# A spatial bias folded into the matmul sum, gating read from PSUM on VectorE, and two buffers moved

## The chip, the cores and the metric

The kernel runs on one core of a Trainium2 chip. The metric is the device time of one execution in microseconds (us); lower is better. The engines are TensorE (PE in the rows, its weight loads PEld), VectorE (DVE), ScalarE (ACT), GpSimd (POOL) and SyncE (SP), which issues nearly all DMAs. Each engine works through its own instructions in the order in which the program gives them.

## The reference, cut to what matters

An mLSTM attention over 2 batches of 768 tokens feeds a gated layer, and that a channel mix. The change is in the gated layer (bias and gating) and at the start of the channel mix:

```
h = np.maximum(x @ w_in, 0.0)
u, v = h[..., :512], h[..., 512:]
v_n = (v - mean) / np.sqrt(var + 1e-06)
v_s = np.einsum('ts,bsd->btd', w_spatial, v_n) + b_spatial[None, :, None]
x = (u * v_s) @ w_out                       # the gated layer's output
xk = mu_k * x + (1.0 - mu_k) * x_prev       # x_prev: x one token earlier
xr = mu_r * x + (1.0 - mu_r) * x_prev
k = np.maximum(xk @ w_k, 0.0)
out = sigmoid(xr @ w_r) * ((k * k) @ w_v)
```

## The kernel before

All products are made of rounded 32-bit pairs: a value is split into a high part and the rest (the low part), and a product is the sum of high by high, high by low and low by high. So each tensor on its way to TensorE needs a cast (ScalarE) and a subtraction of the cast (VectorE or GpSimd).

**Stages.** Until about 134 us attention, w_in products (`vp`, `up`) and normalising (`vn`) are interleaved. Then comes the stage of the change. The tokens are worked on in four groups g = 0 to 3 (batch b = g // 2, half hf = g % 2, 384 tokens each):

- `spatial(g, d)`, four times per group (d = 0 to 3): 18 products `spp` of 128x384 into one PSUM bank. They read `vn` of the batch and `wsp` of the half. Then VectorE adds the bias (L999) and so empties the bank, GpSimd multiplies by `u` (L1000), ScalarE casts (L1001) and VectorE subtracts; the results are the two halves of a `gt` tile.
- `wout(g)`: 32 products `wop`, three result banks, which are copied into `x2_g` (L1017 to L1020). The result for f = 2 comes first, and its copy is L1018.
- `mixed(g, w, ...)`: the token mix of `x2_g` into a buffer `tm`, and its split into `xk` (w = 0) or `xr` (w = 1).
- `kpart(g, f, xk)`: 8 products `kp`, with a chain of ScalarE (relu), GpSimd (square), ScalarE (cast), VectorE (rest); then 24 products `rp` (sigmoid), then 72 products `vv`, and the output.

**Order on TensorE.** Line 1084 sets it: group 0's `spp`, group 1's, `wop` of 0, `spp` of 2, `wop` of 1, `spp` of 3, `wop` of 2, then 32 `kp` of group 0, `wop` of 3, 32 more `kp`, `rp`, `vv`, and then groups 1 to 3 of the channel mix.

**Order on the other engines.** A planner (`Chain`, `advance`, `issue`) issues the steps of each chain when its own clock says that they can start; the second entry of a step is its assumed length in us. Those numbers set only the order. The weights w_k, w_r, w_v and the second half of w_spatial come by DMA into a few raw slots, and are split there (`widen`: three VectorE steps, two of ScalarE, one of GpSimd per piece; a piece of w_spatial needs only a cast and a subtraction). The raw slots are two of tag `wraw`, and after attention one of the three `xt` slots.

**Buffers.** Twelve pages of tag `pg` hold in turn `vn`, `wk`, `x2_g` and `tm`: which page a new tile takes follows from the order in which the program asks for pages and gives them up, and its first writer waits until the last reader of the old tile is through. `gk` slots (11) hold `gt` and later `k2`. A `vn` of a batch is two pairs of pages: chunks 0 to 2, which the first nine of each 18 products read, and chunks 3 to 5.

Of the kernel before, what the change touches and what calls it, by code (L numbers as in the profile page):

```python
# [7 lines left out]
F32 = mybir.dt.float32  # L8
# [9 lines left out]
def tile_mlstm_gmlp_channelmix(  # L18
# [56 lines left out]
    done = {}  # L75
    back = []
    split = []
    raws = dict(wraw=0, xt=0)
    rawcap = dict(wraw=2, xt=0)
    owners = {}  # L80

    class Chain:
# [87 lines left out]
    def chain(key, *steps, ready=None):  # L170
        running.append(Chain(key, steps, clock[0] + 0.2 if ready is None else ready, 0.0))
# [59 lines left out]
    def sub(eng, out, a, b):  # L231
        eng.tensor_tensor(out=out, in0=a, in1=b.bitcast(F32), op=ALU.subtract)  # L232
# [9 lines left out]
    def raw_slot(n):  # L242
        tag = [t for t in raws if raws[t] < rawcap[t]][0]
        raws[tag] += 1
        return base.tile([P, 5 * 128 if tag == "xt" else 512], I64, tag=tag, name="wraw",
                         bufs=3 if tag == "xt" else 2)[:, :n], tag

    def widen(key, hi, lo, src=None, raw=None, ready=0.0):
        n = (raw if src is None else src).shape[-1]
        u = n / 512.0  # L250
        t = {}
        me = (key, next(ids))

        def fetch():
            t["raw"], t["tag"] = raw_slot(n)
            load_end[0] = load(t["raw"], src, n)

        def low():
            for o, sl in lo if isinstance(lo, tuple) else ((lo, slice(0, n)),):
                sub(pool, o, t["sq"][:, sl], hi[:, sl])  # L260
            split.remove(me)

        def s1():
            split.append(me)
            pair = (t["raw"] if raw is None else raw).bitcast(I32).rearrange("p (n two) -> p n two", two=2)
# [25 lines left out]
    def rows3(t, w):  # L291
        return t[:, :3 * w].rearrange("p (a b) -> p a b", a=3)
# [682 lines left out]
    sync.dma_start(out=b_sb, in_=b_sp)  # L975
    x2 = {}
    gts = {}

    def run(prs, out, after, first=(), cost=0.16):
        for t in mm3([out], prs, after, first, cost):  # L980
            t[0]()

    def spatial(g, d):
        b, hf = divmod(g, 2)
        prs = []
        for s in range(NCH):
# [17 lines left out]
        run(prs, mm_bank(f"spp{g}_{d}", ("sp", g, d))[:, :HF], after, [f"w_sp{hf}"] + [("vn", NCH * b + s) for s in range(NCH)])  # L1004
# [88 lines left out]
    def kpart(g, f, xk):  # L1093
        sl = slice((f % 4) * P, (f % 4 + 1) * P)

        def after(ps):
            own("sq", 3, ("k2", g, f))
            sq = rk.tile([P, HF], F32, tag="sq", name=f"sq{g}_{f}", bufs=3)
            t = gated(f"k2_{g}_{f}")
            chain(("k2", g, f), ("A", 0.37, lambda: act.activation(out=sq, in_=ps, func=AF.Relu), ("kp", g, f)),  # L1100
                  ("P", 0.96, lambda: pool.tensor_tensor(out=sq, in0=sq, in1=sq, op=ALU.mult)),  # L1101
                  ("A", 0.41, lambda: act.copy(t[:, 0], sq)), ("V", 0.47, lambda: sub(vec, t[:, 1], sq, t[:, 0])))  # L1102
            k2t[g, f] = t

        run(pairs320(xparts(xk, slice(0, HF)), wparts(wk[f // 4], sl), swap=True),
            mm_bank(f"kp{g}_{f}", ("kp", g, f))[:, :HF], after, [("mx", g, 0), f"w_k{f // 4}"])

    xk = xks[0]
    for g in range(2 * B):
# [8 lines left out]
        for j in range(3):  # L1118
            sl = slice(j * P, (j + 1) * P)
            own("rs", 3, ("ob", g, j))  # L1120
            rs = r2.tile([P, DM], F32, tag="rs", name=f"rs{g}_{j}", bufs=3)
            run(pairs320(xparts(xr, sl), wparts(wr, slice(0, DM))), mm_bank(f"rp{g}_{j}", ("rs", g, j))[:, :DM],
                lambda ps, rs=rs, j=j: chain(("rs", g, j), ("A", 0.35, lambda: act.activation(out=rs, in_=ps, func=AF.Sigmoid))),
                [("mx", g, 1), "wr"], 0.133)
            rss.append(rs)
        for j in range(3):
            sl = slice(j * P, (j + 1) * P)
# [6 lines left out]
            def after(ps):  # L1134
# [113 lines left out]
```

## Time and profile before

| | us |
|---|---|
| median of 3 runs | 331.29 (330.44 to 336.69) |
| profiled execution, own time | 327.45 |
| its span, first to last instruction | 325.7 |
| TensorE busy in the span | 302.4 |
| VectorE, ScalarE, GpSimd busy | 224.3, 163.2, 145.6 |

The profiled execution is one run of its own; it was 3.84 us under the median of the three timed runs. Busy time of TensorE counts the overlap of its pipelined products, so a stretch in which it is always busy can still be slow where the granted clock is low.

### The profile page before, as it was taken

What the parts mean: (1) busy time and instruction counts of PE and PEld (TensorE: products, weight loads), DVE (VectorE), ACT (ScalarE), POOL (GpSimd) and SP (SyncE); (2) the same over time, 40 slices, a digit from 0 to 9 for tenths busy, and PEclk for the clock granted to TensorE, in tenths of its full rate; (3) what the DMA queues carried; (4) which work ended last, traced back from release to release, by engine and by line L of the source; (5) the groups of instructions that cost most, each with busy time, mean ns of one, the idle gap of its engine ahead of it and who ended that gap; (6) DMA issues with size and microseconds to landing.
All of it is one profiled execution on the core that took longest, in us unless ns stands there. A gap on an engine that the chain in (4) does not pass through costs nothing.

```text
span 325.7 us, 5486 instructions
## 1 busy us (share of the span) xinstructions
PE 302.4 (93%) x1982; PEld 281.5 (86%) x1982; DVE 224.3 (69%) x430; ACT 163.2 (50%) x336; POOL 145.6 (45%) x185
## 2 busy tenths in 40 slices
PE   5979988999999999899999999449999999999995
PEld 3676866989989989799999999339999999999995
DVE  6679698958689656654997929996565745645611
ACT  4542644685466342742455316458874844753620
POOL 4133457935758644853464631655502502501500
PEclk9969997999999999999999999987999999999999
DMA  5763942353443213244115211410001001001001
GB/s 181 248 174 124 344 135 85 109 169 105 163 132 112 84 49 104 89 155 139 42 40 193 83 40 40 122 42 2 0 22 41 2 20 40 2 20 42 0 20 42
DMA packets 12854, 28.97 MB, mean 89 GB/s; under 512 B 2099, under 2 KB 6187, under 8 KB 12827
## 3 DMA queue, kind: packets, MB, share of 16 engines
q1 hardware_dynamic: 12795, 28.56, 27.5%
q8 instruction: 16, 0.26, 0.3%
q14 instruction: 11, 0.09, 0.1%
q0 software_dynamic: 32, 0.07, 0.1%
HBM read 26.35 MB, written 1.97 MB: 87 GB/s over the span
## 4 chain that ended last, share of the span: by engine, by line
PE 74%; DVE 10%; ACT 5%; POOL 4%; DMA 3%; issue 2%; SPq 1%; DVEq 0%; ACTq 0%; POOLq 0%
PE spp L612 14%; PE vv L612 13%; PE kp L612 12%; PE vp L612 6%; PE wop L612 5%; PE up L612 5%; PE av L541 5%; PE rp L612 4%; PE sc L444 3%; DMA w_inv<-in_w_in_dram 2%; PE ld L453 2%; DVE wbits L274 2%; PE wp L348 2%; PE ip L525 2%; PE sp L491 1%
## 5 line engine op out<-in xcount | busy, mean ns | idle before, releaser
L1101 POOL TENSOR_TENSOR sq<-sq 128x384 f32<-128x384 f32 x32 | 27.2, 852 | 60.3 <-ACT sq L1100 60.3
L612 PE MATMUL spp<-wsp,vn 128*128 128x384 f32 x288 | 51.0, 335 | 1.5 <-POOL vn L232 0.9
L612 PEld LDWEIGHTS spp<-wsp,vn 128*128 128x128 f32 x288 | 49.8, 188 | 2.2 <-POOL vn L232 1.2
L612 PE MATMUL kp<-xk,wk 128*128 128x384 f32 x256 | 45.9, 336 | 4.6 <-DVE vs L999 4.6
L612 PEld LDWEIGHTS kp<-xk,wk 128*128 128x128 f32 x256 | 44.4, 188 | 5.2 <-DVE vs L999 5.2
L612 PE MATMUL vv<-wv,k 128*128 128x320 f32 x288 | 43.4, 310 | 0.1
L612 PEld LDWEIGHTS vv<-wv,k 128*128 128x128 f32 x288 | 42.4, 188 | 0.6 <-DVE k L232 0.3
L232 DVE TENSOR_TENSOR k<-sq,k 128x384 fp32r<-128x384 f32 x32 | 25.7, 802 | 21.7 <-ACT k L1102 21.7
L612 PE MATMUL vp<-w_v,xg 128*128 128x512 f32 x96 | 29.3, 422 | 2.3 <-ACT xg L603 1.4
L612 PE MATMUL up<-xg,w_u 128*128 128x256 f32 x192 | 31.2, 293 | 0.0
L612 PE MATMUL wop<-gt,wo 128*128 128x384 f32 x128 | 25.7, 358 | 4.5 <-DVE vs L999 2.9
L612 PEld LDWEIGHTS wop<-gt,wo 128*128 128x128 f32 x128 | 24.1, 203 | 5.7 <-ACT wv L285 3.2
L1000 POOL TENSOR_TENSOR vs<-vs,u 128x384 f32<-128x384 f32 x16 | 20.5, 1281 | 14.2 <-DVE vs L999 14.2
L612 PEld LDWEIGHTS up<-xg,w_u 128*128 128x128 f32 x192 | 26.2, 190 | 0.5
L541 PEld LDWEIGHTS av<-kvq,dt 128*128 128x128 f32 x192 | 25.7, 203 | 0.7
L541 PE MATMUL av<-kvq,dt 128*128 128x41 f32 x192 | 25.3, 284 | 0.0
L1100 ACT ACTIVATE sq<-kp 128x384 f32<-128x384 f32 x32 | 15.4, 491 | 15.4 <-PE kp L612 15.4
L274 DVE SCALAR_TENSOR_TENSOR wbits<-wsq,wbits 128x320 int32<-128x320 int32 (+1 forms) x27 | 21.3, 793 | 2.5 <-ACT wsq L269 2.1
L612 PEld LDWEIGHTS vp<-w_v,xg 128*128 128x128 f32 x96 | 17.5, 194 | 5.8 <-DVE xg L232 1.5
L466 DVE TENSOR_TENSOR dt<-dt,sc 128x512 f32<-128x512 f32 x24 | 16.2, 682 | 7.7 <-ACT dt L463 4.5
L1140 DVE TENSOR_TENSOR ob<-rs,vv 128x320 f32<-128x320 f32 x12 | 5.8, 487 | 20.7 <-PE vv L612 20.7
L463 ACT ACTIVATE dt<-ld 128x512 f32<-128x512 f32 x24 | 14.1, 597 | 9.2 <-PE ld L455 6.1
(160 smaller groups left out, 560.3 us busy)
## 6 DMA issues: line engine op xcount, KB each, us to landing
kvq<-in_kvq_dram SPq DMA_DIRECT2D x10, 516.0 KB
qk<-in_qk_dram SPq DMA_DIRECT2D x24, 160.0 KB
wraw<-in_w_k_dram SPq DMA_DIRECT2D x6, 512.0 KB
wraw<-in_w_v_dram SPq DMA_DIRECT2D x8, 320.0 KB
wraw<-in_w_sp_dram SPq DMA_DIRECT2D x12, 192.0 KB
og<-in_o_tok_dram SPq DMA_DIRECT2D x4, 480.0 KB
out_dram<-ob SPq DMA_DIRECT2D x12, 160.0 KB
w_inv<-in_w_in_dram SPq DMA_DIRECT2D x3, 512.0 KB
```

The source lines that it names most:

```text
L232: eng.tensor_tensor(out=out, in0=a, in1=b.bitcast(F32), op=ALU.subtract)
L274: vec.scalar_tensor_tensor(out=t["bits"], in0=t["sq"].bitcast(I32), scalar=3, in1=t["bits"], op0=ALU.logical_shift_left, op1=ALU.bitwise_or)
L348: pe.matmul(wp[:, :256], junk[:, :P], junk, start=True, stop=True)
L444: pe.matmul(st["sc", i, x][:, h * P:(h + 1) * P], k_[64 * x:64 * x + D, h, :], q_[64 * x:64 * x + D, h, :], start=True, stop=True)
L453: pe.matmul(ld, lts[c % 2][:, b], rl[:, hh * 512:(hh + 1) * 512], start=True, stop=not early)
L463: ("A", 0.48, lambda: act.activation(out=d2, in_=ld, func=AF.Exp), ("e", i, hh)),
L466: ("V", 0.6, lambda: vec.tensor_tensor(out=d2, in0=d2, in1=sc, op=ALU.mult)))
L541: pe.matmul(av[:, 4 * hh + h, :], A[:, h, :], vt[:, 4 * hh + h, :], start=True, stop=True)
L612: pe.matmul(out[0], l, x, start=j == 0, stop=j == len(prs) - 1)
L1000: ("P", 0.96, lambda: pool.tensor_tensor(out=vs, in0=vs, in1=ut[b][:, d, sl], op=ALU.mult)),
L1100: chain(("k2", g, f), ("A", 0.37, lambda: act.activation(out=sq, in_=ps, func=AF.Relu), ("kp", g, f)), ("P", 0.96, lambda: pool.tensor_ten ...
L1101: ("P", 0.96, lambda: pool.tensor_tensor(out=sq, in0=sq, in1=sq, op=ALU.mult)),
```

## The change

1. **Bias as a product.** `bm` (128 x 768) is a copy of the broadcast bias rounded by ScalarE; in its lower 64 partitions VectorE puts the rest (bias minus rounded bias). `sel` is a 128x128 tile of 1/64. One more product, `sel` by `bm`, ends the sum of each `spatial(g, d)`: 64 times 1/64 of the rounded bias plus 64 times 1/64 of the rest. There are 16 such products, 19 in each sum instead of 18.
2. **Gating on VectorE.** The bias addition (L999) and the multiplication on GpSimd (L1000) go; VectorE multiplies the PSUM bank by `u` instead.
3. **The mixing buffer.** `tm` of group 0, w = 0 takes the third `xt` slot instead of a page. Each page after it shifts by one: before, `x2_1` took the first page of batch 1's `vn`; now it takes a page of batch 0's `vn`, and `x2_2` the first page of batch 1's.
4. **The raw slot.** The third raw slot moves from tag `xt` to a slot of its own (`rraw`) in the pool `rk`, and takes the space of one `gk` slot (10 instead of 11). The bias arrives in a `gk` slot.
5. **Estimates.** The planner's assumed lengths are set to other numbers, and so the order on VectorE, ScalarE, GpSimd and SyncE shifts.

```
-    rawcap = dict(wraw=2, xt=0)
+    rawcap = dict(wraw=2, xt=0, rraw=0)
...
+        if tag == "rraw":
+            return late_pool[0].tile([P, 512], I64, tag=tag, name="wraw", bufs=1)[:, :n], tag
...
-        v = 0.06 + 0.54 * u
+        v = 0.06 + (1.06 if closing else 0.54) * u
...
-    rawcap["xt"] = 1
+    rawcap["xt"] = 0
...
+    rawcap["rraw"] = 1
...
-        return rk.tile([P, 2, HF], F32R, tag="gk", name=name, bufs=11)
+        return rk.tile([P, 2, HF], F32R, tag="gk", name=name, bufs=10)
...
-    b_sb = r1.tile([P, S], F32, name="b_sb")
+    b_sb = gated("b_sb").rearrange("p w t -> p (w t)").bitcast(F32)
+    bm = r1.tile([P, S], F32R, name="bm")
+    sel = r1.tile([P, P], F32R, name="sel")
     sync.dma_start(out=b_sb, in_=b_sp)
+    pool.memset(sel.bitcast(F32), 1.0 / 64)
+    act.copy(bm, b_sb)
+    sub(vec, bm[64:], b_sb[64:], bm[64:])
...
             prs += [(v0, w0), (v0, w1), (v1, w0)]
+        prs.append((sel, bm[:, hf * HF:(hf + 1) * HF]))
...
-                  ("V", 0.47, lambda: vec.tensor_tensor(out=vs, in0=ps, in1=b_sb[:, sl], op=ALU.add), ("sp", g, d)),
-                  ("P", 0.96, lambda: pool.tensor_tensor(out=vs, in0=vs, in1=ut[b][:, d, sl], op=ALU.mult)),
-                  ("A", 0.41, lambda: act.copy(gt[:, 0], vs)), ("V", 0.47, lambda: sub(vec, gt[:, 1], vs, gt[:, 0])))
+                  ("V", 0.55, lambda: vec.tensor_tensor(out=vs, in0=ps, in1=ut[b][:, d, sl], op=ALU.mult), ("sp", g, d)),
+                  ("A", 0.51, lambda: act.copy(gt[:, 0], vs)), ("V", 0.7, lambda: sub(vec, gt[:, 1], vs, gt[:, 0])))
...
-        t = rows3(page(f"tm{g}_{w}", F32, keys=[("mx", g, w)]), HF)
+        t = xslot(f"tm{g}_{w}", 3 * HF).bitcast(F32) if (g, w) == (0, 0) else page(f"tm{g}_{w}", F32, keys=[("mx", g, w)])
+        t = rows3(t, HF)
```

**Where the instructions stand.** The names in the rows are those of the program with buffer numbers behind; `spp_0` is the sum for d = 0, `x_1` is `x2_1`, `wop_2` the result for f = 2, `tm_0` the mixing buffer for w = 0. TensorE, end of the first sum of group 0 and start of the second, before:

```order
L612 MATMUL spp_0_1785<-wsp_1_1040,vn_0_1302 128x384 x2
L612 MATMUL spp_0_1785<-wsp_1_1040,vn_1_1303 128x384
L612 MATMUL spp_1_1821<-wsp_0_1039,vn_0_491 128x384 x2
L612 MATMUL spp_1_1821<-wsp_0_1039,vn_1_492 128x384
L612 MATMUL spp_1_1821<-wsp_0_1039,vn_0_491 128x384 x2
```

The same place on TensorE in the changed kernel:

```order
L616 MATMUL spp_0_1790<-wsp_1_1040,vn_0_1302 128x384 x2
L616 MATMUL spp_0_1790<-wsp_1_1040,vn_1_1303 128x384
L616 MATMUL spp_0_1790<-bm,sel 128x384
L616 MATMUL spp_1_1823<-wsp_0_1039,vn_0_491 128x384 x2
L616 MATMUL spp_1_1823<-wsp_0_1039,vn_1_492 128x384
```

The bias product stands between the first sum and the second. It waits for VectorE (`bm`) and for GpSimd (`sel`), and everything behind it on TensorE stands in its queue.

VectorE at the same time, before, from the last `vr` of the normalising to the first `gt`:

```order
L679 TENSOR_SCALAR vr_1708<-vr_1708,sb_1709 128x512
L232 TENSOR_TENSOR wsp_0_1783<-wraw,wsp_0_1783 128x384 x2
L999 TENSOR_TENSOR vs_0_1816<-spp_0_1785,b_sb 128x384
L232 TENSOR_TENSOR wsp_0_1783<-wraw,wsp_0_1783 128x384
L232 TENSOR_TENSOR wsp_1_1784<-wraw,wsp_1_1784 128x384 x2
L232 TENSOR_TENSOR gt_0_1817<-vs_0_1816,gt_0_1817 128x384
```

VectorE there in the changed kernel:

```order
L683 TENSOR_SCALAR vr_1708<-vr_1708,sb_1709 128x512
L233 TENSOR_TENSOR bm<-b_sb,bm 64x768
L233 TENSOR_TENSOR wsp_0_1788<-wraw,wsp_0_1788 128x384
L1016 TENSOR_TENSOR vs_0_1818<-spp_0_1790,u_841 128x384
L233 TENSOR_TENSOR wsp_0_1788<-wraw,wsp_0_1788 128x384 x2
L233 TENSOR_TENSOR gt_0_1819<-vs_0_1818,gt_0_1819 128x384
```

The rest of the bias is made right behind the last `vr`, ahead of all `wsp` pieces. On ScalarE the cast of `bm` stands likewise behind the last cast of `vn` and ahead of the `wsp` casts.

ScalarE around the copy of group 1's first `wop` result, before:

```order
L1001 CAST gt_2_2211<-vs_2_2210 128x384
L1037 ACTIVATE tm_0_2245<-x_0_2036,omu_sb 128x384 x2
L1018 COPY x_1_2246<-wop_2_2247 64x384
L1037 ACTIVATE tm_0_2245<-x_0_2036,omu_sb 128x384
L1001 CAST gt_3_2241<-vs_3_2240 128x384
L1020 COPY x_1_2246<-x_1_2246 64x384
L1017 COPY x_1_2246<-wop_0_2267 128x384
L269 ACTIVATE wsq<-wraw 128x320
L1044 CAST xk_2244<-tm_0_2245 128x1152
```

ScalarE there in the changed kernel:

```order
L1017 CAST gt_2_2204<-vs_2_2203 128x384
L272 ACTIVATE wsq<-wraw 128x512
L1055 ACTIVATE tm_0_2243<-x_0_2039,omu_sb 128x384 x2
L1034 COPY x_1_2244<-wop_2_2245 64x384
L1017 CAST gt_3_2239<-vs_3_2238 128x384
L1055 ACTIVATE tm_0_2243<-x_0_2039,omu_sb 128x384
L1033 COPY x_1_2244<-wop_0_2260 128x384
L1036 COPY x_1_2244<-x_1_2244 64x384
L1033 COPY x_1_2244<-wop_1_2279 128x384
L289 CAST wk_0_2100<-wsq 128x512
L1062 CAST xk_2242<-tm_0_2243 128x1152
```

The copy into `x_1` stands at nearly the same place in the queue; what has moved is its page, and with it the tile whose readers it waits for.

## Rows read from the trace of the kernel before

**Rows 1.** Busy time by stretch, all engines: PE, PEld, DVE, ACT, POOL, granted clock, DMA share.

```profile
185.00:196.00 11.00, 11.00 (x65) 11.00 (x64) 4.23 (x5) 2.73 (x6) 5.02 (x4) 1.00 0.17 54
196.00:212.00 16.00, 11.44 (x65) 10.80 (x64) 15.34 (x28) 8.85 (x18) 6.32 (x7) 1.00 0.28 82
```

**Rows 2.** Timeline of TensorE, 125 to 250: start, length, line, operation, count, [idle before, releaser].

```profile
138.75 22.30 PE L612 MATMUL spp<-wsp,vn 128*128 128x384 f32 x127 [0.87 <-POOL vn L232]
...
166.44 12.64 PE L612 MATMUL spp<-wsp,vn 128*128 128x384 f32 x72
178.92 5.71 PE L612 MATMUL wop<-gt,wo 128*128 128x384 f32 x32
184.46 12.64 PE L612 MATMUL spp<-wsp,vn 128*128 128x384 f32 x72
...
202.49 2.94 PE L612 MATMUL kp<-xk,wk 128*128 128x384 f32 x16
207.37 1.69 PE L612 MATMUL kp<-xk,wk 128*128 128x384 f32 x8 [1.95 <-DVE vs L999]
211.67 1.68 PE L612 MATMUL kp<-xk,wk 128*128 128x384 f32 x8 [2.61 <-DVE vs L999]
216.29 1.72 PE L612 MATMUL wop<-gt,wo 128*128 128x384 f32 x6 [2.94 <-DVE vs L999]
218.66 0.69 PE L612 MATMUL wop<-gt,wo 128*128 128x384 f32 x1 [0.64 <-ACT gt L1001]
220.27 6.19 PE L612 MATMUL wop<-gt,wo 128*128 128x384 f32 x25 [0.93 <-DVE gt L232]
...
231.84 3.67 PE L612 MATMUL rp<-wr,xr 128*128 128x320 f32 x24
```

**Rows 3.** Timeline of VectorE, 125 to 250.

```profile
195.92 0.55 DVE L1019 TENSOR_TENSOR x<-x,wop 64x384 f32<-64x384 f32 x1 [6.77 <-ACT x L1018]
...
202.65 0.56 DVE L999 TENSOR_TENSOR vs<-spp,b_sb 128x384 f32<-128x384 f32 x1
...
215.60 0.55 DVE L999 TENSOR_TENSOR vs<-spp,b_sb 128x384 f32<-128x384 f32 x1
```

**Rows 4.** Timeline of ScalarE, 125 to 250.

```profile
140.49 0.62 ACT L681 CAST vn<-vr 128x512 fp32r<-128x512 f32 x1 [1.88 <-DVE vr L679]
141.02 1.34 ACT L731 CAST wsp<-wraw 128x384 fp32r<-128x384 f32 x3
...
195.41 0.48 ACT L1018 COPY x<-wop 64x384 f32<-64x384 f32 x1 [6.69 <-PE spp L612]
```

**Rows 5.** Busy time by stretch around the bias load, columns as in Rows 1.

```profile
139.20:140.60 1.40, 1.40 (x10) 1.40 (x9) 0.95 (x1) 0.11 (x1) 1.40 (x3) 1.00 0.94 343
140.60:141.90 1.30, 1.30 (x9) 1.30 (x9) 0.34 (x1) 1.30 (x4) 0.75 (x2) 1.00 0.00 0
```

**Rows 6.** Timeline of SyncE's DMA issues, 134 to 143.

```profile
138.00 0.43 SPq L975 DMA_DIRECT2D b_sb<-in_b_sp_dram  x1
```

**Rows 7.** Timeline of GpSimd, 125 to 250.

```profile
141.19 1.31 POOL L232 TENSOR_TENSOR vn<-vr,vn 128x512 fp32r<-128x512 f32 x1 [0.55 <-ACT vn L681]
```

**Rows 8.** The tile wsp from 115 to 152: durations min/median/max in ns.

```profile
L232 DVE TENSOR_TENSOR wsp<-wraw,wsp x6: 546/554/1350, 141.6 to 147.8; 128x384 fp32r<-128x384 f32 x6
```

**Rows 9.** Groups of instructions, shapes kept apart: count, busy us, mean ns of one.

```profile
L1000 POOL TENSOR_TENSOR vs<-vs,u 128x384 f32<-128x384 f32 x16 | 20.5, 1281 | 14.2 <-DVE vs L999 14.2
...
L999 DVE TENSOR_TENSOR vs<-spp,b_sb 128x384 f32<-128x384 f32 x16 | 8.8, 548 | 0.1
L1001 ACT CAST gt<-vs 128x384 fp32r<-128x384 f32 x16 | 8.2, 511 | 12.0 <-POOL vs L1000 12.0
...
L1044 ACT CAST xk<-tm 128x1152 fp32r<-128x1152 f32 x4 | 4.6, 1157 | 2.3 <-DVE tm L1040 2.3
...
L232 DVE TENSOR_TENSOR xk<-tm,xk 128x768 fp32r<-128x768 f32 x4 | 3.8, 958 | 3.8 <-ACT xk L1044 3.7
```

**Rows 10.** Busy TensorE by stretch: length, PE busy, granted clock, DMA share.

```profile
53.10:56.50 3.40, 3.40 (x21) 0.50 0.01 3
...
216.90:220.30 3.40, 1.83 (x6) 0.50 0.02 7
220.30:223.70 3.40, 3.40 (x11) 0.50 0.00 0
```

More of the change, by code (lines that the diff above doesn't have):

```diff
@@ L77, in tile_mlstm_gmlp_channelmix @@
     split = []
-    raws = dict(wraw=0, xt=0)
-    rawcap = dict(wraw=2, xt=0)
+    raws = dict(wraw=0, xt=0, rraw=0)
+    rawcap = dict(wraw=2, xt=0, rraw=0)
+    late_pool = []
     owners = {}
@@ L281, in s3 @@
                 raws[t["tag"]] -= 1
-        v = 0.06 + 0.54 * u
-        steps = [("V", 0.12 + 0.54 * u, s1, None, lambda: len(split) < 2), ("V", v, s2), ("V", v, s3),
+        v = 0.06 + (1.06 if closing else 0.54) * u
+        steps = [("V", 0.12 + (0.84 if closing else 0.54) * u, s1, None, lambda: len(split) < 2), ("V", v, s2), ("V", v, s3),
                  ("A", 0.16 + 0.36 * u, lambda: act.copy(hi, t["sq"])), ("P", 0.1 + 1.13 * u, low)]
@@ L964, in tile_mlstm_gmlp_channelmix, with run @@
     at.release()
-    rawcap["xt"] = 1
+    rawcap["xt"] = 0
     rk = tc.alloc_tile_pool(name="rk", bufs=1, side="right", reuse_waits="tile")
+    late_pool.append(rk)
+    rawcap["rraw"] = 1
     def gated(name):
-        return rk.tile([P, 2, HF], F32R, tag="gk", name=name, bufs=11)
+        return rk.tile([P, 2, HF], F32R, tag="gk", name=name, bufs=10)
     r1 = tc.alloc_tile_pool(name="r1", bufs=1, side="right", reuse_waits="tile")
-    b_sb = r1.tile([P, S], F32, name="b_sb")
+    b_sb = gated("b_sb").rearrange("p w t -> p (w t)").bitcast(F32)
+    bm = r1.tile([P, S], F32R, name="bm")
+    sel = r1.tile([P, P], F32R, name="sel")
     sync.dma_start(out=b_sb, in_=b_sp)
+    pool.memset(sel.bitcast(F32), 1.0 / 64)
+    act.copy(bm, b_sb)
+    sub(vec, bm[64:], b_sb[64:], bm[64:])
+    use("A", 0.85)
+    use("V", 0.9)
     x2 = {}
     gts = {}
-    def run(prs, out, after, first=(), cost=0.16):
+    def run(prs, out, after, first=(), cost=0.173):
         for t in mm3([out], prs, after, first, cost):
@@ L1041, in blend @@
                                                     in1=t[:, c], op0=ALU.mult, op1=ALU.add)
-        chain(("mx", g, w), *[("A", 0.5, keep(c)) for c in range(3)], *[("V", 0.53, blend(c)) for c in range(3)],
-              ("A", 1.05, lambda: act.copy(xt[:, 0:3], t)),
-              ("V", 0.87, lambda: sub(vec, xt[:, 3:5], t[:, 0:2], xt[:, 0:2])),
+        chain(("mx", g, w), *[("A", 0.6, keep(c)) for c in range(3)], *[("V", 0.62, blend(c)) for c in range(3)],
+              ("A", 1.16, lambda: act.copy(xt[:, 0:3], t)),
+              ("V", 0.96, lambda: sub(vec, xt[:, 3:5], t[:, 0:2], xt[:, 0:2])),
               ("V", 0.47, lambda: sub(vec, xt[64:, 2], t[64:, 2], xt[64:, 2])),
@@ L1099, in after @@
             t = gated(f"k2_{g}_{f}")
-            chain(("k2", g, f), ("A", 0.37, lambda: act.activation(out=sq, in_=ps, func=AF.Relu), ("kp", g, f)),
+            chain(("k2", g, f), ("A", 0.49, lambda: act.activation(out=sq, in_=ps, func=AF.Relu), ("kp", g, f)),
                   ("P", 0.96, lambda: pool.tensor_tensor(out=sq, in0=sq, in1=sq, op=ALU.mult)),
-                  ("A", 0.41, lambda: act.copy(t[:, 0], sq)), ("V", 0.47, lambda: sub(vec, t[:, 1], sq, t[:, 0])))
+                  ("A", 0.51, lambda: act.copy(t[:, 0], sq)), ("V", 0.62, lambda: sub(vec, t[:, 1], sq, t[:, 0])))
             k2t[g, f] = t
@@ L1123, in tile_mlstm_gmlp_channelmix @@
                 lambda ps, rs=rs, j=j: chain(("rs", g, j), ("A", 0.35, lambda: act.activation(out=rs, in_=ps, func=AF.Sigmoid))),
-                [("mx", g, 1), "wr"], 0.133)
+                [("mx", g, 1), "wr"], 0.147)
             rss.append(rs)
@@ L1145, in tile_mlstm_gmlp_channelmix @@
             run(prs, mm_bank(f"vv{g}_{j}", ("ob", g, j))[:, :DM], after,
-                ["wv"] + [("k2", g, f) for f in range(8)], 0.133)
+                ["wv"] + [("k2", g, f) for f in range(8)], 0.147)
     finish(*[c.key for c in running])
```

## The prediction

> **What bounds the kernel now.** I read the busy time by stretch first, then the timelines of TensorE, VectorE and ScalarE, then the rows around the bias load. TensorE is the engine that works nearly all the time, and where it works without waits its products follow each other at 12.48 us for 72, or 0.1733 us each (from 166.44 to 178.92) [rows 2]. So a change is worth what it takes from TensorE's waits and from stretches at the low clock, less the products that it adds.
>
> One place holds nearly all of the waits after attention. From 202.49 to 231.84 TensorE does 32 `kp`, 32 `wop` and 32 `kp`: 96 products, which at 0.1733 are 16.6 us, in 29.35 us. So 12.7 us are lost there: 1.95 + 2.61 + 2.94 + 0.64 + 0.93 = 9.1 us of waits, and 3.6 us for a slower pace, most of it between 216.9 and 223.7, where the granted clock is at 0.5, that is 1.2 GHz [rows 2, 10]. The three long waits name VectorE's `vs` (L999): it is the instruction that empties the PSUM banks of group 3.
>
> Why is VectorE late? Group 3's first sum is done at about 187.6 (184.46 + 18 products), but its `vs` comes at 202.65, and the fourth at 215.60 [rows 3]. In 196 to 212 VectorE is busy for 15.34 us of 16; in 185 to 196 for only 4.23 of 11 [rows 1]. In between it waits for 6.77 us, up to 195.92, for a copy on ScalarE, and that copy (L1018, into `x2_1`) waits for 6.69 us, up to 195.41, for an `spp` product [rows 3, 4]. Its own source, the first result of `wop` of group 1, was there at about 180.3 (178.92 + 8 products). From 184.46 to 195.41 are 10.95 us, or 63 products: three sums of 18 and nine more, the last product that reads the first `vn` page of batch 1. So the copy waits for its page, not for its data, and with it stand both queues, ScalarE's and VectorE's. The jam at 205 to 220 is this stop, paid later.
>
> **The change, part by part.**
>
> The mixing buffer. With `tm` on an `xt` slot, `x2_1` takes a page of batch 0's `vn`, whose last reader is in group 1's sums, before `wop` of group 1; `x2_2` takes the page that `x2_1` had, and is written after group 3's sums. So the stop of 6.7 us goes. Does all of the 12.7 us go with it? VectorE starts the queue of group 3 some 6.8 us earlier, while TensorE comes to its `kp` some 8.7 us later than before (the three costs below). That is 15 us against 9.1 us of waits, so I take the whole 12.7. Its cover is thus 6 us; if that were gone, the waits would come back one for one. What is late next is nothing of this stage: `kp`, `rp` and `vv` run on TensorE's own pace.
>
> Gating. Sixteen additions of 548 ns on VectorE become sixteen multiplications that likewise read one operand from PSUM: nothing either way. Sixteen steps of 1281 ns leave GpSimd, 20.5 us [rows 9]. None is on TensorE's path while its waits come from VectorE's queue; the step shortens the way from a sum to its `gt` by 1.3 us, hidden behind at least one other group's sums. I cost it at nothing.
>
> The bias products. 16 x 0.1733 = 2.8 us, all on TensorE and covered by nothing.
>
> The wait for `bm`. This is the new one. The bias product ends the first sum of group 0, and behind it on TensorE stand all the other sums; behind TensorE, VectorE's `vs` and all after it. The 18th product of that sum starts at 138.75 [rows 2], so the 19th could start at 138.9. But the bias is only asked for at 138.00 [rows 6], behind raw pieces in SyncE's queue whose slots come free as before. Its transfer lies in the stretch to 140.6, where the DMA share is 0.94; after that it is 0.00 [rows 5]. ScalarE is then still at the last cast of `vn` and free for the cast of `bm` at 141.02 [rows 4]. A cast takes 511 ns for 384 columns and 1157 for 1152, so about 0.83 for 768: to 141.85 [rows 9]. VectorE's subtraction has 768 columns, like the one of `xk` at 958 ns [rows 9]: alone it would end at 142.9. But GpSimd works on `vn` from 141.19 to 142.50 [rows 7], and the `wsp` subtraction that stood at this very place took 1350 ns where its like take 554 [rows 8]; it ended at 142.9, 0.4 us behind GpSimd's step. If the longer one of `bm` is held in the same way it ends at about 143.3. I take 143.3, since that row is the same operation at the same place: a wait of 4.4 us, with bounds 3.9 and 4.6. `sel` is set on GpSimd behind the `vn` step and is there earlier. The GPSIMD Engine Reference of the Trainium skill (section 1, Specifications) says that GpSimd shares its way into SBUF with VectorE, in contention with VectorE instructions that have two SBUF inputs; the row of 1350 ns agrees. By it the new gating, with one input in PSUM, is never held, while `bm` is; without it the sum would be 0.4 us better.
>
> The clock. Idle times of 1.95, 2.61 and 2.94 us close together ended in a low stretch of 6.8 us, the two rows from 216.9 to 223.7 [rows 2, 10]. The new idle time is longer than any of these and comes 0.2 us behind one of 0.87 us, so I expect the clock to fall around 142 to 143. In 220.3 to 223.7 TensorE did 11 products in 3.4 us where 1.9 us would do: 1.5 us lost [rows 10]. A low stretch of only 3.4 us stands at 53.1 to 56.5, with TensorE busy all through [rows 10]. As TensorE here has no further wait behind `bm`, that row is the nearest: I take 1.5 us, with bounds 0 and 3.0. The Trainium skill (TensorE: Matmul & The Clock Gate, section Terms) puts the price at half of the low time, 1.7 us for such a stretch; the sum would then be 0.2 us worse.
>
> Raw slot, `gk` slots, estimates. With the third raw slot taken later, most pieces of the second half of w_spatial are split between 142 and 148. They are needed by group 1's sums, which now begin at 143.3 + 58 x 0.1733 = 153.4: covered by some 5 us. Of ten `gk` slots at most nine are in use before `wop` of group 0. Nothing for either.
>
> Sum: 12.7 - 2.8 - 4.4 - 1.5 = 4.0 us faster. The same from the timeline: TensorE goes on at 143.3, does 478 products to the first `rp`, 82.8 us, and 1.5 for the clock: 227.6, against 231.84. The profiled execution would go from 327.45 to 323.4; the median of the runs shown lies 3.84 above it, and I carry the difference over: 331.29 - 4.0 = 327.3 us.
>
> **The rivals.**
>
> (a) The clock doesn't fall, or while TensorE still waits: net 12.7 - 2.8 - 4.4 = 5.5, so 325.8. For it speaks that the wait of 0.87 us at 138 left it at 1.0 [rows 2, 5]; against it the length of this one.
>
> (b) VectorE stays behind. The stop of 6.7 us goes, but its queue in 143 to 210 is now interleaved by other estimates, and each `vs` that stands behind a split piece of w_k or w_v holds a bank. It decides once VectorE runs more than the 6 us of cover late at group 3. With half of the 12.7 us left, the time is 331.29 - 4.0 + 6.35 = 333.6, slower than before; with all of it 340.0. For it speaks VectorE's 15.34 us of 16 in rows 1; against it that this was a backlog and that 20.5 us of GpSimd steps, beside which its subtractions were held, are gone.
>
> (c) The page isn't what holds the copy, and the stop stays: then the three costs, 8.7 us, come on top, less the 4.4 us by which TensorE comes to the `kp` later because of `bm`: about 335.6. The count of 63 products speaks against it.
>
> (d) The timed runs of before lose more at 205 to 220 than the profiled one; their median is 3.84 us higher. If all of that lay there, the gain would be 7.8: 323.5.
>
> **How the numbers follow.** Chances: forecast 0.50 (own range 325.9 to 329.0), (a) 0.20, (b) 0.12, (c) 0.03, (d) 0.15. A measurement of this kernel can tell about 2%, 6.6 us, from no change, so the border lies at 324.7. (d) and a small part of (a) are below it: 0.19 faster; the worse part of (b) is above 337.9: 0.05 slower; the rest, 0.76, is within. The range leaves out (b) and (c), 0.15 together, and the tail of (d): 323.0 to 332.5.
>
> **What would show it.** In the changed kernel's profile: TensorE idle at about 138.9 to 143.3, released by VectorE's `bm`; the granted clock at 0.5 behind it; no wait of ScalarE on `spp` at 188 to 195; VectorE's `vs` of group 3 within 2 us of its sums; no waits of TensorE between the first `kp` and `rp`, and `rp` of group 0 at about 227.6. I would be wrong if `bm` were ready before 139, if the `kp` stage still waited for VectorE, or if the low clock lasted longer than 6.8 us.

## The result, and the profile after

Over 20 executions of each, the changed kernel takes 328.13 us in the median (322.63 to 332.78), the kernel before 331.17 (326.00 to 337.46). The ratio is 0.9869, with a 95% interval of 0.9828 to 0.9911: 1.3% faster, less than the 2% that a measurement here can tell from no change. The ratios leave disturbed executions out, the medians hold all of them. The prediction was 327.3 us, 4.0 less than before; by the medians it is 3.0 less.

The profiled execution of the changed kernel took 325.98 us, with a span of 324.2. Before `spp` the two programs do the same, yet the first `spp` starts at 135.89 instead of 133.85; the granted clock is at 0.5 for 17.1 us ahead of it instead of 10.2. So I compare from the first `spp` on: 188.31 us to the end of the span instead of 191.85.

The timeline of TensorE in the changed kernel, which answers to [rows 2]:

```profile
135.89 2.77 PE L616 MATMUL spp<-wsp,vn 128*128 128x384 f32 x15
139.30 0.61 PE L616 MATMUL spp<-wsp,vn 128*128 128x384 f32 x2 [0.64 <-ACT vn L685]
140.79 0.44 PE L616 MATMUL spp<-wsp,vn 128*128 128x384 f32 x1 [0.87 <-POOL vn L233]
145.67 0.66 PE L616 MATMUL spp<-bm,sel 128*128 128x384 f32 x1 [4.44 <-DVE bm L233]
...
151.52 3.28 PE L616 MATMUL spp<-wsp,vn 128*128 128x384 f32 x18
...
214.27 5.71 PE L616 MATMUL kp<-xk,wk 128*128 128x384 f32 x32
219.81 5.71 PE L616 MATMUL wop<-gt,wo 128*128 128x384 f32 x32
225.36 5.71 PE L616 MATMUL kp<-xk,wk 128*128 128x384 f32 x32
230.91 3.67 PE L616 MATMUL rp<-wr,xr 128*128 128x320 f32 x24
```

From the first `kp` to `rp` it is now 16.64 us without a wait, instead of 29.35: 12.7 us less. From the first `spp` to the first `kp` it is 78.38 instead of 68.64: 9.74 more. That is the 16 products, 2.8, the one wait for `bm`, 4.7 (4.88 from the start of the 18th product to that of the 19th, less one product; the row's 4.44 counts the idle time alone), and the clock: from 145.67 to 151.52 there are 20 products in 5.85 us, where 3.47 would do, so 2.4 lost. The three make 9.9, within 0.2 of the 9.74. From `rp` to the end it is 0.6 less, all in the first `vv`. So 12.71 - 9.74 + 0.57 = 3.54 us are gained from the first `spp` on.

The busy times by stretch of the changed kernel; columns as in [rows 1]:

```profile
143.85:150.68 6.83, 5.01 (x16) 5.04 (x17) 4.39 (x8) 3.80 (x8) 0.77 (x2) 0.50 0.29 90
...
185.00:196.00 11.00, 11.00 (x65) 11.00 (x64) 8.80 (x16) 6.12 (x13) 2.52 (x2) 1.00 0.25 79
196.00:212.00 16.00, 16.00 (x94) 16.00 (x93) 11.43 (x25) 7.68 (x15) 4.36 (x4) 1.00 0.26 82
```

The clock stands at 0.5 for 6.83 us behind the wait. VectorE has 8.80 and 11.43 us of work where [rows 1] had 4.23 and 15.34: the stop and the jam are both gone.

How the bias came in the changed kernel, its timelines of SyncE, ScalarE, GpSimd and VectorE, and on ScalarE and VectorE the rows that answer to [rows 3, 4]:

```profile
140.09 0.38 SPq L986 DMA_DIRECT2D b_sb<-in_b_sp_dram  x1
140.56 7.67 SPq L214 DMA_DIRECT2D wraw<-in_w_sp_dram  x4
```

```profile
142.51 0.62 ACT L685 CAST vn<-vr 128x512 fp32r<-128x512 f32 x1 [1.87 <-DVE vr L683]
143.70 0.83 ACT L988 CAST bm<-b_sb 128x768 fp32r<-128x768 f32 x1 [0.57 <-DMA b_sb<-in_b_sp_dram]
...
191.59 0.47 ACT L1034 COPY x<-wop 64x384 f32<-64x384 f32 x1 [0.91 <-PE wop L616]
```

```profile
143.21 1.27 POOL L233 TENSOR_TENSOR vn<-vr,vn 128x512 fp32r<-128x512 f32 x1 [0.55 <-ACT vn L685]
```

```profile
144.57 0.96 DVE L233 TENSOR_TENSOR bm<-b_sb,bm 64x768 fp32r<-64x768 f32 x1 [2.09 <-ACT bm L988]
...
202.33 0.56 DVE L1016 TENSOR_TENSOR vs<-spp,u 128x384 f32<-128x384 f32 x1 [0.96 <-PE spp L616]
```

The cast takes 0.83 us as worked out, but waits 0.57 for the transfer. SyncE now asks for the next piece of w_spatial right behind the bias, at 140.56; before, that request came at 142.94, 4.9 us behind the bias. The moved raw slot is the likely reason for both, as the two transfers then share the DMA engines (their share is 0.96 at 142.5 to 143.0), but no run separates it. The subtraction takes 0.96 and isn't held: GpSimd's `vn` step ended at 144.48, 0.1 us before it starts. The copy into `x2_1` (191.59) waits for its own `wop` result, and VectorE waits for group 3's sums instead of the other way round.

### The profile page after: what moved, and what is told of

Its sections match the earlier page's. It is cut to its first block, busy times and chain, and to the rows that moved or that the text cites. A ratio compares the mean times of both kernels' runs of the same rounds, so it can differ in the third digit from the quotient of the medians.

```text
span 324.2 us, 5500 instructions
## 1 busy us (share of the span) xinstructions
PE 304.9 (94%) x1998; PEld 285.4 (88%) x1998; DVE 216.8 (67%) x431; ACT 163.7 (51%) x337; POOL 126.8 (39%) x170
## 4 chain that ended last, share of the span: by engine, by line
PE 80%; DMA 6%; DVE 5%; ACT 3%; POOL 2%; issue 1%; SPq 1%; ACTq 0%; DVEq 0%
PE spp L616 16%; PE kp L616 14%; PE vv L616 13%; PE wop L616 7%; PE vp L616 7%; PE up L616 5%; PE rp L616 4%; PE av L545 4%; DMA kvq<-in_kvq_dram 3%; PE sc L448 3%; DMA qk<-in_qk_dram 2%; PE wp L352 2%; PE ld L457 2%; PE ip L529 2%; PE sp L495 1%
## 5 line engine op out<-in xcount | busy, mean ns | idle before, releaser
L616 PE MATMUL spp<-wsp,vn 128*128 128x384 f32 x288 | 55.1, 344 | 1.5 <-POOL vn L233 0.9
L616 PEld LDWEIGHTS spp<-wsp,vn 128*128 128x128 f32 x288 | 52.3, 195 | 2.1 <-POOL vn L233 1.2
L1119 POOL TENSOR_TENSOR sq<-sq 128x384 f32<-128x384 f32 x32 | 28.1, 880 | 54.8 <-ACT sq L1118 54.8
L616 PE MATMUL vp<-w_v,xg 128*128 128x512 f32 x96 | 30.1, 433 | 2.8 <-ACT xg L607 1.4
L545 PEld LDWEIGHTS av<-kvq,dt 128*128 128x128 f32 x192 | 24.8, 197 | 1.6 <-ACT nn L565 0.9
L233 POOL TENSOR_TENSOR wk<-wsq,wk 128x512 fp32r<-128x512 f32 x6 | 7.8, 1306 | 41.9 <-ACT wk L289 34.0
L616 PEld LDWEIGHTS vp<-w_v,xg 128*128 128x128 f32 x96 | 18.2, 201 | 6.2 <-DVE xg L233 1.7
L616 PE MATMUL wop<-gt,wo 128*128 128x384 f32 x128 | 22.8, 334 | 0.0
L277 DVE SCALAR_TENSOR_TENSOR wbits<-wsq,wbits 128x320 int32<-128x320 int32 (+1 forms) x27 | 19.3, 717 | 4.6 <-ACT wsq L272 4.3
L616 PEld LDWEIGHTS wop<-gt,wo 128*128 128x128 f32 x128 | 22.2, 188 | 0.0
```

The source lines that it names most:

```text
L545: pe.matmul(av[:, 4 * hh + h, :], A[:, h, :], vt[:, 4 * hh + h, :], start=True, stop=True)
L616: pe.matmul(out[0], l, x, start=j == 0, stop=j == len(prs) - 1)
```

## The experiments

Theory: the page of `x2_1` made the jam, and the bias gives back most of what its end brings. Rivals: the gating or the estimates ended the jam; the costs of the bias are hidden.

All fourteen kernels in one table, worked out from each profile: start of the first `spp` and of the first `rp` in the timeline of TensorE, and the span. "Kp stage" is from the first `kp` to `rp`, 16.64 without a wait. "Slack" is the start of the first `vv` less that of GpSimd's last w_v step; that step takes about 1.1 us, and its result is read only by the 22nd product of `vv`, 21 x 0.147 = 3.1 us on, so 2 us come on top. The last column is the ratio to before with its interval; many of the intervals overlap, so I read the places from the profiles.

| kernel | first spp | spp to rp | kp stage | rp to end | spp to end | waits in first rp and vv | slack | ratio to before |
|---|---|---|---|---|---|---|---|---|
| before | 133.85 | 97.99 | 29.35 | 93.86 | 191.85 | 0 | 14.0 | 1 |
| changed | 135.89 | 95.02 | 16.64 | 93.29 | 188.31 | 0 | 1.1 | 0.9869 (0.9828 to 0.9911) |
| e1 moves alone | 135.96 | 91.53 | 21.30 | 93.91 | 185.44 | 0 | 14.0 | 0.9788 (0.9718 to 0.9858) |
| e2 tm on a page | 136.60 | 100.09 | 21.73 | 102.11 | 202.20 | 4.5 | -4.7 | 1.0239 (1.0164 to 1.0314) |
| e3 two sums as before | 138.89 | 89.26 | 16.64 | 93.35 | 182.61 | 0 | 1.1 | 0.9649 (0.9585 to 0.9713) |
| e4 no bias | 140.97 | 85.27 | 16.65 | 95.76 | 181.03 | 2.0 | -4.5 | 0.9577 (0.9509 to 0.9645) |
| e5 old estimates | 135.13 | 94.11 | 16.64 | 93.26 | 187.37 | 0 | 21.9 | 0.9868 (0.9770 to 0.9966) |
| e6 estimates alone | 140.87 | 93.54 | 24.91 | 101.89 | 195.43 | 4.8 | -9.1 | 1.0259 (1.0096 to 1.0422) |
| e7 moves, estimates | 138.75 | 86.83 | 16.64 | 100.02 | 186.85 | 4.0 | -7.7 | 0.9851 (0.9774 to 0.9929) |
| e8 moves, VectorE gating | 138.82 | 86.08 | 17.45 | 98.80 | 184.88 | 2.6 | 7.7 | none; median 323.37 |
| e9 moves, both | 133.36 | 86.83 | 16.64 | 104.61 | 191.44 | 6.0 | -11.1 | 0.9899 (0.9823 to 0.9975) |
| e10 as e3, old estimates | 133.63 | 89.25 | 16.64 | 93.32 | 182.57 | 0 | 21.7 | 0.9660 (0.9616 to 0.9703) |
| e11 8 products, old estimates | 141.26 | 86.65 | 16.64 | 95.09 | 181.74 | 1.2 | 14.9 | 0.9682 (0.9612 to 0.9751) |
| e12 8 products, new estimates | 138.90 | 86.65 | 16.64 | 94.65 | 181.30 | 0.8 | -3.4 | 0.9661 (0.9596 to 0.9726) |

**e1: the kernel before with the buffer moves alone.**

```
-        t = rows3(page(f"tm{g}_{w}", F32, keys=[("mx", g, w)]), HF)
+        t = xslot(f"tm{g}_{w}", 3 * HF).bitcast(F32) if (g, w) == (0, 0) else page(f"tm{g}_{w}", F32, keys=[("mx", g, w)])
+        t = rows3(t, HF)
...
-        return rk.tile([P, 2, HF], F32R, tag="gk", name=name, bufs=11)
+        return rk.tile([P, 2, HF], F32R, tag="gk", name=name, bufs=10)
```

The third raw slot goes to `rk` as in the change.

> The kernel before with the buffer moves alone (mixing buffer of group 0 on an xt slot, third raw slot in rk, ten gk slots); bias addition, gating on GpSimd and estimates stay as before. Theory, the page alone ends the jam: ScalarE's copy into x2_1 waits for its wop result only, TensorE has no long waits between its first kp and rp (12.7 us less there), and about 318.5 us, a ratio of 0.962 to before. Rival, the gating or the estimates are needed too: the first VectorE instruction of group 3 still comes late, several us of waits in the kp stage stay, 324 to 331 us.

326.09 us, ratio 0.9788. The theory held half. The copy into `x2_1` no longer waits for an `spp`, but the kp stage is still 4.66 us too long. Timelines of ScalarE and TensorE in e1:

```profile
190.78 0.48 ACT L1024 COPY x<-wop 64x384 f32<-64x384 f32 x1
```

```profile
206.19 5.71 PE L615 MATMUL kp<-xk,wk 128*128 128x384 f32 x32
211.92 1.28 PE L615 MATMUL wop<-gt,wo 128*128 128x384 f32 x6
214.30 0.44 PE L615 MATMUL wop<-gt,wo 128*128 128x384 f32 x1 [1.10 <-ACT gt L1007]
215.92 6.19 PE L615 MATMUL wop<-gt,wo 128*128 128x384 f32 x25 [1.17 <-DVE gt L233]
221.94 5.71 PE L615 MATMUL kp<-xk,wk 128*128 128x384 f32 x32
```

So the moves alone bring 8.05 of the 12.7 us. Of the 4.66 that stay, 2.27 are waits for `gt` (1.10 and 1.17), and the rest is a slower pace, most of it behind the second wait. Two rows of e1's VectorE, and GpSimd beside them:

```profile
199.10 1.14 DVE L273 TENSOR_SCALAR wbits<-wraw 128x320 int32<-128x320 int32 x1
...
201.25 0.31 DVE L273 TENSOR_SCALAR wbits<-wraw 128x320 int32<-128x320 int32 x1
```

```profile
198.93 1.13 POOL L1006 TENSOR_TENSOR vs<-vs,u 128x384 f32<-128x384 f32 x1 [1.15 <-DVE vs L1005]
200.02 0.96 POOL L233 TENSOR_TENSOR wv<-wsq,wv 128x320 fp32r<-128x320 f32 x1
```

The same shift takes 0.31 us alone and 1.14 when it starts beside GpSimd's gating. The Trainium skill (SBUF — State Buffer, section SBUF: two separate sides) calls the port pair that the two engines share an exclusive lock: between a GpSimd instruction and a VectorE one that has two SBUF inputs or is in a 2-port mode, the one that starts first has it for its whole instruction. The rows fit: the shift of 199.10 ends at 200.24, 0.2 us behind the gating's end at 200.06. That this shift, with one input, is in such a mode no row says.

**e2: the changed kernel with `tm` of group 0 back on a page.**

```
-        t = xslot(f"tm{g}_{w}", 3 * HF).bitcast(F32) if (g, w) == (0, 0) else page(f"tm{g}_{w}", F32, keys=[("mx", g, w)])
+        t = page(f"tm{g}_{w}", F32, keys=[("mx", g, w)])
```

> The changed kernel with one line undone: the mixing buffer of group 0 is back on a page, so that x2_1 falls again on the first vn page of batch 1; bias product, gating and estimates stay. Theory, the page is the cause: ScalarE waits some 6 to 7 us for an spp product of group 3, TensorE waits 8 us or more at its kp and wop, and the time is 7 to 13 us above the changed kernel, 335 to 341 us. Rival, the gating on VectorE and the new estimates already end the jam: ScalarE's wait stays but TensorE's don't come, 327 to 330 us.

339.32 us, ratio 1.0239: 3.7% over the changed kernel by the two ratios, for one line. The stop is back, and longer than expected. ScalarE and VectorE in e2:

```profile
207.70 0.47 ACT L1034 COPY x<-wop 64x384 f32<-64x384 f32 x1 [16.34 <-PE spp L616]
```

```profile
208.75 0.56 DVE L233 TENSOR_TENSOR gt<-vs,gt 128x384 fp32r<-128x384 f32 x1 [16.70 <-ACT gt L1017]
```

TensorE in e2, the first of group 3's sums:

```profile
196.24 3.28 PE L616 MATMUL spp<-wsp,vn 128*128 128x384 f32 x18
```

Three sums of 19 products and nine more are 66, or 11.44 us: to 207.68, and the copy starts at 207.70. The count of the prediction, which there gave 63 products, holds again. [Rows 4] had 6.69, up to 195.41. The end of the wait is 12.3 us later, since TensorE comes later to group 3's sums, while ScalarE is at the copy only 2.6 us later (207.70 - 16.34 = 191.36 against 188.72). And the loss comes at other places: in the kp stage 5.1 us, behind `rp` 8.8, for w_k, `xr` and `k`.

**e3: the first two sums of group 0 as before, 14 bias products.**

```
+        added = g == 0 and d < 2
+        if not added:
             prs.append((sel, bm[:, hf * HF:(hf + 1) * HF]))
...
+                  *([("V", 0.55, lambda: vec.tensor_tensor(out=vs, in0=ps, in1=b_sb[:, sl], op=ALU.add), ("sp", g, d)),
+                     ("P", 0.96, lambda: pool.tensor_tensor(out=vs, in0=vs, in1=ut[b][:, d, sl], op=ALU.mult))] if added else
```

> The changed kernel with the first two sums of group 0 as before (bias added on VectorE, gating on GpSimd, no bias product), the other 14 with the bias product: TensorE need not wait for bm. Theory: the wait of 4.4 us and the 2.4 us at the low clock go, and two products (0.35 us): 7.2 us less, about 321 us, no wait of TensorE over 1 us at the end of the first sum. Rival, the clock falls anyway or the wait turns up at the bank of the first sum: 2 us or more of this stay, 323 to 328 us.

319.25 us, ratio 0.9649. The wait is gone, and the first bias product comes 37 products later. Timeline of TensorE in e3:

```profile
143.79 8.25 PE L616 MATMUL spp<-wsp,vn 128*128 128x384 f32 x37 [0.86 <-POOL vn L233]
151.88 0.33 PE L616 MATMUL spp<-bm,sel 128*128 128x384 f32 x1
```

From `spp` to `rp` 5.76 us less than in the changed kernel: 4.7 for the wait, 0.35 for two products, 0.7 for the clock. The clock still fell, for 3.4 us behind the two short waits that before has too: the 37 products took 8.09 us to the next one instead of 6.41. So of the 2.4 us only 0.7 hung on the wait for `bm` here.

**e4: no bias product, the bias left out.** The line that appends it is gone.

> The changed kernel without the bias product in any sum, so the bias is left out of the computation (it is still loaded and split). Theory: 16 products of 0.1733 us (2.8), the wait of 4.4 us and 2.4 us of low clock go, 9.6 us less than the changed kernel, about 318.5 us, and no more than the kernel before with the buffer moves alone. Rival, part of the three costs is hidden behind waits that then come back in the kp stage: 321 to 325 us.

320.64 us in the median, 315.69 to 327.96, ratio 0.9577. Up to `rp` it is 9.75 us shorter than the changed kernel, as the theory has it (9.6). But 2.5 us of that come back behind `rp`. TensorE in e4:

```profile
234.20 0.42 PE L616 MATMUL vv<-wv,k 128*128 128x320 f32 x1 [1.21 <-ACT wv L289]
235.38 7.60 PE L616 MATMUL vv<-wv,k 128*128 128x320 f32 x50 [0.77 <-POOL wv L233]
```

The rival named the kp stage; the waits come at `vv`, for the last w_v piece. With the last w_v piece where the changed kernel has it, TensorE could come 3 us earlier before it waits (slack 1.1 and 2). The piece doesn't stay in place, though: in e3 TensorE comes 5.76 us earlier, and the slack is still 1.1.

**e5: the changed kernel with the old estimates.** All numbers of part 5 of the change set back.

> The changed kernel with all of the planner's estimates set back to the old numbers; bias product, gating on VectorE and buffer moves stay. Theory G (the part of the jam that the buffer moves alone left, 4.7 us, went because GpSimd's gating no longer runs beside VectorE): no wait of TensorE over 1 us between its first kp and rp, as in the changed kernel, and 327 to 329 us. Rival E (the new estimates took it away): waits of 2 us or more and a low clock in that stretch, 331 to 334 us.

326.96 us, ratio 0.9868, as the changed kernel, and no waits in the kp stage: theory G's side. VectorE's groups over 185 to 222, first in e1, then in e5, which has the same estimates but no gating on GpSimd:

```profile
L273 DVE TENSOR_SCALAR wbits<-wraw 128x320 int32<-128x320 int32 x8 | 6.0, 746 | 0.2 <-DMA wraw<-in_w_v_dram 0.2
...
L233 DVE TENSOR_TENSOR gt<-vs,gt 128x384 fp32r<-128x384 f32 x7 | 5.3, 754 | 0.1
L277 DVE SCALAR_TENSOR_TENSOR wbits<-wsq,wbits 128x320 int32<-128x320 int32 x8 | 5.0, 627 | 0.1
```

```profile
L273 DVE TENSOR_SCALAR wbits<-wraw 128x320 int32<-128x320 int32 x8 | 3.9, 503 | 0.9 <-DMA wraw<-in_w_v_dram 0.8
L277 DVE SCALAR_TENSOR_TENSOR wbits<-wsq,wbits 128x320 int32<-128x320 int32 x8 | 3.8, 483 | 0.5 <-ACT wsq L272 0.4
L233 DVE TENSOR_TENSOR gt<-vs,gt 128x384 fp32r<-128x384 f32 x6 | 3.3, 548 | 0.1
```

Eight shifts are 0.24 us shorter, eight others 0.14, seven subtractions 0.21: some 4.5 us of VectorE's time there, near the 4.66 that e1 still lost. That alone doesn't show the cause: TensorE also reaches its first `kp` 7.2 us later here than in e1 (77.47 and 70.23 from the first `spp`). What the new estimates do shows in the slack: w_v's last piece comes 21.9 us before the first `vv` with the old numbers, 1.1 with the new.

**e6: the kernel before with the new estimates alone.**

> The kernel before with the new estimates alone; buffers, bias addition and gating as before. Theory (the page holds ScalarE's copy whatever the order): ScalarE still waits 5 us or more for an spp product of group 3 and VectorE with it, and, since the new estimates also put the w_v pieces later, the loss comes at the kp stage, at vv, or both: from the first spp to the end 190 to 200 us (191.85 before), 330 to 338 us in all. Rival, the estimates alone end the jam: 182 to 187 us from the first spp to the end, 321 to 326 us in all.

337.37 us, ratio 1.0259. The theory held: the copy into `x2_1` waits 9.14 us for an `spp`, until 202.42 (group 3's sums start at 191.48, and 63 products end at 202.40), and the loss is spread over the kp stage (8.3 over 16.64) and what follows `rp`.

**e7: moves and new estimates, gating on GpSimd.**

> The kernel before with the buffer moves and the new estimates; bias addition on VectorE and gating on GpSimd stay. Theory G: TensorE still waits 2 us or more for gt between its first kp and rp, the gt subtraction on VectorE still takes about 750 ns in 185 to 222, about 326 us as with the moves alone. Rival E: no waits over 1 us there and about 321 us.

326.57 us, ratio 0.9851. Neither as stated: no waits in the kp stage, as rival E has it, but the time of theory G, since 4.0 us of waits came at the first `vv`, for w_v and `k`. VectorE empties group 3's banks first and does the w_v pieces later. The `gt` subtractions, which theory G had at 750 ns, are short with the gating still on GpSimd, and the shifts are longer than in e1:

```profile
L273 DVE TENSOR_SCALAR wbits<-wraw 128x320 int32<-128x320 int32 x6 | 5.2, 866 | 0.1
L233 DVE TENSOR_TENSOR gt<-vs,gt 128x384 fp32r<-128x384 f32 x7 | 3.9, 552 | 0.1
```

**e8: moves, gating as a second instruction on VectorE, old estimates.**

```
-                  ("P", 0.96, lambda: pool.tensor_tensor(out=vs, in0=vs, in1=ut[b][:, d, sl], op=ALU.mult)),
+                  ("V", 0.47, lambda: vec.tensor_tensor(out=vs, in0=vs, in1=ut[b][:, d, sl], op=ALU.mult)),
```

> The kernel before with the buffer moves and the gating as a second instruction on VectorE (bias added there from PSUM, then multiplied in place), old estimates. Theory G: the gt subtraction comes down from 754 to about 560 ns, TensorE's waits between its first kp and rp are under 1 us in sum, and 321 to 322 us although VectorE has 16 more instructions of some 0.55 us. Rival, VectorE's own load is what counts: its 8.8 us more keep it busy over 15 us of 16 at 196 to 212, the waits stay or grow, 326 us or more.

323.37 us in the median of 316.20 to 325.36, too wide for a ratio. The kp stage waits for 0.51 us, as G has it. But the `gt` subtraction fell only from 754 to 709 ns, without any gating on GpSimd:

```profile
L233 DVE TENSOR_TENSOR gt<-vs,gt 128x384 fp32r<-128x384 f32 x7 | 5.0, 709 | 0.3 <-ACT gt L1007 0.2
```

So G's forecast of the waits holds, and its reason, the shorter subtraction, mostly doesn't. 2.6 us of waits for `k` came in the first `vv`; that VectorE's 16 additional instructions are paid there is likely, but not shown. 184.88 from `spp` to the end is about e1's 185.44, and e1 had lost 1.6 more to a low stretch in `spp`. Whether gating by a further VectorE instruction pays stays open: the two profiles say no, while the shortest of the four executions, 316.20, is below e1's shortest, 322.15.

**e9: moves, VectorE gating and new estimates.** e8 with part 5 of the change.

> The kernel before with the buffer moves, the gating as a second instruction on VectorE and the new estimates: all of the change but the bias product. Theory: no waits in the kp stage, no wait for bm, 16 products fewer than the changed kernel: 9.6 us less than it, about 318.5 us, and 1.5 to 2.5 us less than the version with 14 bias products (319.3). Rival, VectorE's 16 additional instructions bring waits back: 321 us or more.

329.87 us, ratio 0.9899: a miss, and the rival's side. The kp stage is clean, and the first `vv` waits eight times, the clock falling for 10.2 us. Two of the rows of TensorE in e9:

```profile
231.89 0.63 PE L615 MATMUL vv<-wv,k 128*128 128x320 f32 x1 [1.79 <-ACT wv L288]
232.86 0.90 PE L615 MATMUL vv<-wv,k 128*128 128x320 f32 x2 [0.34 <-POOL wv L233]
```

This is all of the change but the bias product, and from `spp` to the end it is 3.1 us slower than the changed kernel: TensorE reaches `vv` earlier, and VectorE, with 16 more instructions, gets to w_v later (slack -11.1).

**e10, e11, e12: fewer bias products, by estimates.** e10 is e3 with the old estimates; in e11 (old) and e12 (new) all sums of groups 0 and 1 are as before, `added = g < 2`.

> The version with the first two sums of group 0 biased and gated as before (14 bias products), now with the old estimates. Theory (the new estimates only put the last w_v pieces later, about 20 us, and take nothing off TensorE's waits once GpSimd's gating is gone from groups 2 and 3): the last w_v piece is split by about 212 instead of 230, no waits between the first kp and rp or in vv, and the same time as with the new estimates, 318 to 320 us. Rival: the old estimates put group 3's gating late again, waits of 2 us or more between the first kp and rp, 321 us or more.

> Old estimates, and all eight sums of groups 0 and 1 biased on VectorE and gated on GpSimd as before; bias products only in groups 2 and 3, 8 instead of 14. Theory (GpSimd's gating costs only where VectorE is behind, at groups 2 and 3): 6 products of 0.1733, 1.0 us less than with 14, 317 to 319 us, no waits of TensorE between the first kp and rp or in vv. Rival: VectorE falls behind in groups 0 and 1 already, waits of 1 us or more in the kp stage, 320 us or more.

> The same with the new estimates. Theory: TensorE is 1.0 us earlier at the first vv than with 14 products, where the last w_v piece was only just in time, so up to 1 us of waits for wv shows in the first vv: 318 to 320 us, and not faster than with the old estimates. Rival: no waits for wv, and the same time as with the old estimates within 0.3 us of profile span from the first spp.

317.71, 319.44 and 320.03 us; ratios 0.9660, 0.9682 and 0.9661, one from the other not told apart. e10 has no waits and w_v early, as expected, at 0.3 us under its range. e12 has 0.77 us of wait for w_v, as expected. e11 isn't as expected: 1.22 us of wait in `vv` for ScalarE's `k`, which I had ruled out; so e12 is not behind it, as forecast, but 0.4 us shorter from `spp` to the end. All three, like e3, beat both kernels, by 1.9 to 2.2% over the changed one by their ratios.

## Why the prediction was right, step by step

**The page: right, and shown both ways.** Moving it, with the raw slot, takes ScalarE's wait away (e1); moving it back alone brings it (e2). Where it waits, it ends where the count of products puts it: 63 in before and e6, 66 in e2.

**"So I take the whole 12.7": right as a sum, only half shown in where it comes from.** 12.7 us went, 8.05 of it with the moves alone (e1). The prediction has TensorE come later to its `kp` to cover what the page leaves. In e1 it comes only 1.6 us later (70.23 us from the first `spp`, 68.64 before). By the prediction's count 9.1 less 6.8 less 1.6, some 0.7 us of waits, would stay; there were 2.27, and 4.66 lost in all. The term that was wrong is the gating that I "cost at nothing": where TensorE comes as early as in e1, moving it away is worth those 4.66 us in the kp stage. e11 shows it, with the old estimates and, in groups 2 and 3, bias products and no gating on GpSimd: it is at the first `kp` after 70.01 us, no later than e1, and doesn't wait in the kp stage. e8, which gates on VectorE, is there after 68.63 and waits for 0.51. Whether the changed kernel, 8 us later at its `kp`, would have needed this, no run shows.

How the gating on GpSimd costs time is open too. Held VectorE steps are one way (rival (b) named them, without a price in the sum), but which steps are held follows from the order: the `gt` subtractions take 754 ns in e1, 552 in e7 with the same gating, and 709 in e8 without it. The other way is the step of 1.3 us between a sum and its `gt`, which the prediction took as hidden. The new estimates also clear the kp stage (e7), but carry the loss to `vv`; beside the new gating they aren't needed (e5).

**"What is late next is nothing of this stage": true, with little to spare.** Take the bias away, and the first `vv` waits for w_v (e4). The cover that I counted, 6 us at group 3, wasn't the smallest.

**The products, 2.8: right. The wait for `bm`, 4.4 against 4.7: a little too small.** The forecast's 4.4 runs from 138.9 to 143.3, where the 19th product could start and where it does; counted in the same way it was 4.7, just over the bound of 4.6. The way there was another, too. The transfer was 0.57 us late for the cast, and so the subtraction came behind GpSimd's step instead of beside it. With that the wait is 0.3 us longer than with the hold that I forecast. That the moved raw slot costs nothing, as the sum has it, is therefore doubtful. The rule that the new gating, with one input in PSUM, is never held agrees with the trace: its 16 took 556 to 559 ns, the one at 202.33 beside a GpSimd step from 201.64 to 202.94.

**The clock, 1.5 against 2.4: mis-sized.** I took a stretch of 3.4 us as the nearest row; with the wait for `bm` it was 6.8 us in all three profiles (the changed kernel, e2, e5). Without it, behind the same two short waits, it was 3.4 us in five profiles and none in six. The low stretch of [rows 10] that followed waits, 6.8 us too, would have been the nearer row.

**The total: near, in part by luck.** The wait and the clock cost 1.2 us more than forecast, so the same sum gives 2.8 instead of 4.0. 0.57 us behind `rp`, in the first `vv`, make up about half of that; no term had them, and no run shows where they come from.

**Rivals.** (a) didn't come: the clock fell. (b) didn't either. (c), the page isn't the cause, fell with e2, which also shows that its price was wrong: I took 4.4 us off because TensorE comes later, but the page is held until TensorE is done with it, so a later TensorE makes the stop longer. (d), that the timed executions of before lose more at the kp stage, was not tested. The first `spp` starts between 133.36 and 141.26 in the profiles, in unchanged code; that alone is more than the 3.84 us by which I had to carry the profiled time to the median.

## What to carry to other kernels

When an engine waits for a matmul whose result it doesn't read, look at the page it writes to: counting the readers from the end of the wait found it here, and moving buffers took 2.1% off (e1), while the new order alone made the kernel 2.6% slower (e6). A change that lets the busiest engine arrive earlier can bring the next deadline into view, here the last w_v piece (e4), so look up the slack there before adding the gains. A new operand should first be needed in a sum that comes after it is ready: adding the bias in the old way for the first two of 16 sums turned 1.3% into about 3.5%.

## What I had not expected of the hardware

The same instructions before `spp` took up to 7.9 us longer in one kernel's profile than in another's: the first `spp` started at 133.36 in e9 and at 141.26 in e11. In e4, where it started at 140.97, the granted clock stood at 0.5 from 50.4 to 70.9; in before, at 133.85, from 18.9 to 25.8 and from 53.1 to 56.5. A shift on VectorE with one SBUF input, 0.31 us alone, took 1.14 beside GpSimd's gating, so not only instructions with two inputs are held.
